# Loading the first rows of x in fewer, taller transfers, and the order of the first norms

## The chip, the cores and the metric

One core of one Trainium2 chip runs the whole kernel in one launch. The metric is the device time of one execution in microseconds (us); the median of three runs of the kernel before is 931.47 us (931.18 to 931.98).

## What is computed

A block of 2048 positions by 512 channels, in float32, goes through two sublayers, each normed, modulated and added back. `B_x` and the inputs' batch of one play no part.

```
mod = (silu(c) @ w_mod).reshape(1, 6, 1, 512)          # sa, ca, ga, sb, cb, gb
h = layernorm(x) * (1 + ca) + sa
a, b = h @ hid_re.T, h @ hid_im.T                      # DFT over the channels
x = x + ga * (seq_re @ a - seq_im @ b)                 # DFT over the positions, real part
h = layernorm(x) * (1 + cb) + sb
z = gelu(h @ w_in)                                     # 512 -> 1792, halves z1 and z2
g = w_sp @ layernorm(z2) + b_sp                        # over the positions
x = x + gb * ((z1 * g) @ w_out)
```

The two 2048 x 2048 matrices of the DFT over the positions, `seq_re` and `seq_im`, are 16 MB each and come from the chip's main memory, as does `x` (4 MB).

## The kernel before, in words

**Precision.** Products are made in a reduced float32 form. Each operand is split in a high part (a copy by ScalarE) and a low part (a difference by VectorE), and three TensorE products (lines 97 to 99) stand for one. The very first step alone (`n` = 0) uses whole float32 operands, line 543, which the profile shows as two passes for each product.

**The first stage.** The order of the sublayer is turned round: the DFT over the positions comes first, on the normed rows. `mm_a(n)`, line 533, is one step of it. For 512 output positions `t`, for the real or the imaginary matrix `j`, and for one tile `s` of 128 rows of x, it adds four products (one for each 128 channels) to four accumulators. Steps 0 to 31 belong to `t` = 0. They take the tiles in groups of four: steps 0 to 3 are the real matrix with tiles 0 to 3, steps 4 to 7 the imaginary one with the same tiles, steps 8 to 15 the tiles 4 to 7, and so on to tile 15. 

**Blocks.** The matrices come in blocks of 512 x 512 (1 MB, tile `stage`, two buffers), one for every four steps. `load` (line 165) issues each block as four transfers of 32 partitions on the sync queue. VectorE turns a quarter of a block by 32 x 32 squares into `t` (line 190). `prep(n)` (line 194) runs two things ahead of the step: `prep_hi(n + 3)`, which turns quarter n + 3 and has ScalarE copy its high part (line 269), and `prep_lo(n + 2)`, in which VectorE makes the low part of quarter n + 2 (line 287). When the last quarter of block b has been turned, block b + 2 is issued.

**Rows of x.** Tile 4g + k holds, in partition 32a + i, row 512g + 128a + 32k + i, to match the turned squares. `load_x` (line 422) brings several k of a group g with one transfer for each a, of 32 partitions. The first two tiles have their own function, `load_two` (line 450): four transfers of 32 partitions for each tile, two issued by the sync queue and two by ScalarE's queue. The first block's first half is issued by the two queues as well, line 161.

**First norms.** `stats_first` (line 436) takes mean and variance on VectorE (lines 439 to 442), the inverse root on GpSimd (line 443), and the product of the two on VectorE for tile 0 and on GpSimd for the others (line 445). `whole_first` (line 458) has ScalarE write tile 0 normed, its channels regrouped, in one activation (line 461), and then a column of ones (line 464). `hi_first` (line 480) writes the high part of a normed tile directly, `norm_x` and `lo_h` give its low part. `keep_busy` (line 365) gives TensorE three float32 products without use while nothing has arrived.

**Order.** The framework adds the waits; it doesn't change the order. Each engine and each DMA queue takes its instructions in the order in which the lines run, so lines 1081 to 1116 are the order of the start, and from line 1117 on `at(n, f, ...)` puts `f` behind step n: `load_x` for the second half of group 1 behind step 0, group 2 behind step 4, group 3 behind step 8, the columns of `w_mod` (tile `wb`, 1 MB each) behind steps 5 and 12; the statistics of later tiles from step 4 on. Lines 1248 to 1253 run the steps.

Of the kernel before, what the change touches and what calls it, by code (L numbers as in the profile page):

```python
# [8 lines left out]
F32 = mybir.dt.float32  # L9
F32R = mybir.dt.float32r  # L10
AF = mybir.ActivationFunctionType
ALU = mybir.AluOpType

P = 128
# [6 lines left out]
def fnet_gmlp_kernel(  # L21
# [32 lines left out]
    nc = tc.nc  # L54
    S, D = x.shape[1:]
    F2 = w_in.shape[1]
    FH = F2 // 2
    Q = 512
    NQ = S // Q
# [4 lines left out]
    x = x.rearrange("b s d -> (b s) d")  # L64
    out = out.rearrange("b s d -> (b s) d")

    def pool(name, side="left", bufs=1):
        return tc.tile_pool(name=name, bufs=bufs, side=side, reuse_waits="tile")
# [11 lines left out]
    def bank(k, name):  # L80
        return psum.tile([P, 512], F32, tag=f"bank{k}", bufs=1, name=name)
# [75 lines left out]
    def load_half(tile_, a, h, engs=(nc.sync,) * 4):  # L157

        v = a.rearrange("(b j) (a s) -> a j b s", j=32, a=4)
        for q in range(4):  # L160
            engs[q].dma_start(tile_[32 * q:32 * q + 32], v[q][:, :, 64 * h:64 * h + 64])
# [3 lines left out]
    def load(b):  # L165
        if b < len(src):
            stage[b] = blocks.tile([P, 16, P], F32, tag="stage", bufs=2, name=f"stage{b}")
            load_block(stage[b], src[b])
        elif b < len(src) + 2:
            j = b - len(src)  # L170
            XB.append(blocks.tile([P, 4, Q], F32, tag="stage", bufs=2, name=f"xb{j}"))
            for g in range(2):
                nc.sync.dma_start(XB[j][:, 2 * g:2 * g + 2], ht_d[g].rearrange("(k p) t -> p k t", p=P)[:, 2 * j:2 * j + 2])
                for kk in range(2):
                    TT[2 * j + kk, g] = XB[j][:, 2 * g + kk]
        elif 4 * (b - NB0) < NE - N4:
            i, gh = divmod(b - NB0, NQ)
            g, h = divmod(gh, 2)
            p = PROD[i]
            stage[b] = blocks.tile([P, 2, 16, 64], F32, tag="stage", bufs=2, name=f"stage{b}")  # L180
            for r in range(2):
                load_half(stage[b][:, r], s_d[S_OF[p], r, g] if p in S_OF else
                          quad(w_sp, r + (2 if p == 4 else 0), g + (2 if p == 1 else 0)), h)
# [5 lines left out]
    def squares(dst, block, k):  # L189
        nc.vector.transpose(dst.rearrange("p (b i) -> p b i", i=32), block[:, :, 32 * k:32 * k + 32])  # L190
# [31 lines left out]
    def form_t(n):  # L222

        if n < N1:
            gg, p, kk = (n - N2) // 4, (n - N2) // 2 % 2, n % 2
            return TT[2 * p + kk, gg]
        p = YPROD[(n - N1) // 4 % len(YPROD)]
        gg, kk = divmod(n % 4, 2)
        a, b, c, d = TT[kk, gg], TT[2 + kk, gg], TT[kk, 2 + gg], TT[2 + kk, 2 + gg]
        return {6: S2[gg, kk], 7: a if n < N3 else c, 4: b if n < N3 else d, 5: c if n < N3 else a, 3: d if n < N3 else b}[p]  # L230
# [21 lines left out]
    def prep_hi(n):  # L252
        if n >= NE or n in highs:
            return
        highs.add(n)
        if N2 <= n < N4:
            T[n] = form_t(n)
        else:
            b, k = divmod(n, 4) if n < N2 else (NB0 + (n - N4) // 4, (n - N4) % 4)
            if b != NB0:  # L260
                T[n] = blocks.tile([P, Q], F32, tag="t", bufs=2, name=f"t{n}")
            if b == NB0:
                assert n in T
            elif n >= N4:
                squares(T[n], stage[b][:, k % 2], k // 2)
            else:
                squares(T[n], stage[b], k)
        AH[n] = SE[2][:, n - N4] if N4 <= n < N4 + 4 else blocks.tile([P, Q], F32R, tag="ah", bufs=4, name=f"ah{n}")
        nc.scalar.activation(AH[n], T[n], AF.Copy)  # L269
        if not N2 <= n < N4 and k == 3:  # L270
            stage.pop(b)
            if b != NB0:
                load(b + 2)


    def prep_lo(n):
        if n >= NE or n in lows:
            return
        lows.add(n)
        if N2 <= n < N4 and n % 4 == 3:  # L280
            AL[n] = slot(0, f"al{n}", F32R) if slots else zrow[0].tile([P, Q], F32R, tag="z1u", bufs=6, name=f"al{n}")
        elif N4 <= n < N4 + 4:
            AL[n] = slot(9 + n - N4, f"al{n}", F32R)
        else:
            AL[n] = blocks.tile([P, Q], F32R, tag="al", bufs=3, name=f"al{n}")
        t = T.pop(n)
        nc.vector.tensor_tensor(AL[n], t, AH[n].bitcast(F32), op=ALU.subtract)  # L287
# [6 lines left out]
    spool = s1.enter_context(pool("spool", "right"))  # L294
# [7 lines left out]
    ones = cpool.tile([P, P], F32, name="ones")  # L302
# [4 lines left out]
    busy = rows.tile([P, D], F32, tag="row", bufs=6, name="busy")  # L307
# [57 lines left out]
    def keep_busy(n, k):  # L365

        ps = bank(k, "busyp")
        for _ in range(n):
            nc.tensor.matmul(ps, ones, busy, start=True, stop=True)

    def fold_sum(t, w, u):

# [46 lines left out]

    X, XG, LN, NRM, h_hi, h_lo = {}, {}, {}, {}, {}, {}  # L420

    def load_x(g, ks=range(4), eng=nc.sync):

        if g not in XG:
            XG[g] = spool.tile([P, 4, D], F32, tag="x", bufs=2, name=f"x{g}")
        k0, k1 = ks[0], ks[-1] + 1
        v = x.rearrange("(g a k i) d -> g a i k d", g=NQ, a=4, i=32)
        for a in range(4):
            eng.dma_start(XG[g][32 * a:32 * a + 32, k0:k1, :], v[g, a][:, k0:k1, :])
        for k in ks:  # L430
            X[4 * g + k] = XG[g][:, k, :]

    def stats_x(s):
# [2 lines left out]
    def stats_first(s):  # L436

        m = spool.tile([P, 12], F32, tag="first", bufs=4, name=f"first{s}")
        nc.vector.bn_stats(m[:, :6], X[s])
        mv = m[:, 8:]  # L440
        nc.vector.bn_aggr(mv[:, :2], m[:, :6])
        nc.vector.tensor_scalar(mv[:, 1:2], mv[:, 1:2], EPS, None, op0=ALU.add)
        nc.gpsimd.tensor_tensor(mv[:, 2:3], mv[:, 1:2], mhalf, op=ALU.pow)
        eng = nc.gpsimd if s else nc.vector
        eng.tensor_scalar(mv[:, 3:4], mv[:, 0:1], mv[:, 2:3], -1.0, op0=ALU.mult, op1=ALU.mult)
        NRM[s] = mv[:, 2:3], mv[:, 3:4]

    two = (nc.sync, nc.sync, nc.scalar, nc.scalar)

    def load_two(k):  # L450
        if not k:
            XG[0] = spool.tile([P, 4, D], F32, tag="x", bufs=2, name="x0")
        v = x.rearrange("(g a k i) d -> g a i k d", g=NQ, a=4, i=32)
        for a in range(4):
            two[a].dma_start(XG[0][32 * a:32 * a + 32, k, :], v[0, a][:, k, :])
        X[k] = XG[0][:, k, :]

    def whole_first(s):

        LN[s] = spool.tile([P, D], F32, tag="xn", bufs=4, name=f"xn{s}")  # L460
        nc.scalar.activation(LN[s].rearrange("p (k a i) -> p k a i", a=4, i=32),
                             X[s].rearrange("p (a k i) -> p k a i", a=4, i=32), AF.Identity,
                             bias=NRM[s][1], scale=NRM[s][0])
        nc.scalar.activation(LN[s][:, :1], ones[:, :1], AF.Copy)

    def split_first(s):
# [7 lines left out]
    def turn_whole(n):  # L474
        T[n] = blocks.tile([P, Q], F32, tag="t", bufs=2, name=f"t{n}")
        squares(T[n], stage[0], n)
        highs.add(n)
        lows.add(n)
# [23 lines left out]
    def ones_x(s):  # L502
        LN[s] = spool.tile([P, D], F32, tag="xn", bufs=4, name=f"xn{s}")
        nc.gpsimd.memset(LN[s][:, 0:1], 1.0)
# [573 lines left out]
            mm([n])  # L1078


    load_two(0)
    stage[0] = blocks.tile([P, 16, P], F32, tag="stage", bufs=2, name="stage0")
    load_half(stage[0][:, :, :64], src[0], 0, two)
    load_two(1)
    nc.scalar.activation(sc, ones[:, :ND], AF.Silu)
    load_x(0, range(2, 4))
    load_half(stage[0][:, :, 64:], src[0], 1)
    load(1)
    load_x(1, range(2))
    keep_busy(3, 5)  # L1090
    ones_x(1)
    ones_x(2)
    ones_x(3)
    stats_first(0)
    whole_first(0)
    turn_whole(0)
    prep_hi(1)
    stats_first(1)
    prep_lo(1)
    hi_first(1)  # L1100
    stats_first(2)
# [13 lines left out]
    rest_first(0)  # L1115
    lo_h(3)
    at(0, load_x, 1, range(2, 4))
    at(2, load_row)
    at(9, silu_row)
# [31 lines left out]
    for j, turn, weigh, row, fold, hi in ((0, (25, 26, 27, 28), (29, 29, 30, 30), 26, (34, 34, 35, 36), (40, 37, 38, 39)),  # L1151
# [8 lines left out]
        n = weigh[3] + 1  # L1160
# [20 lines left out]
    for t in range(NQ):  # L1181
        n = 8 * NQ * (t + 1)
# [136 lines left out]
    for i, p in enumerate(PROD):  # L1319
        for k in range(8):  # L1320
            n = NB[p] + 2 * k
# [11 lines left out]
    for f in range(NF):  # L1333
        n = N4 + 24 + 8 * f
# [109 lines left out]
```

## Time and profile before

| | us |
|---|---|
| median of three runs | 931.47 |
| the profiled execution's own time | 931.31 |
| its span, first to last instruction | 929.5 |
| TensorE products, busy | 923.6 |
| VectorE busy | 736.4 |
| ScalarE busy | 408.7 |
| GpSimd busy | 198.6 |

The profile is one execution; its times are counted from the start of its span. PE is TensorE's products, PEld its weight loads, DVE VectorE, ACT ScalarE, POOL GpSimd, SP the sync engine; a q behind a name is that engine's queue, with the DMA issues. A row of the timeline is start, duration, engine, line, operation, output and inputs; the brackets at its end are the time the engine stood idle before it and what ended that. In the DMA view a queue's row is its packets, the MB it moved and the time of its packets as a share of sixteen DMA engines over the window; an issue's row ends with the median us from issue to landing. A DMA share over 1 means that packets overlap on an engine.

### The profile page before, as it was taken

To read this page: it belongs to the slowest core of one execution; us is meant where nothing else is said; L and a number is where in the kernel's file an instruction comes from. 1 tells how busy PE (TensorE), PEld (TensorE's weight loads), DVE (VectorE), ACT (ScalarE), POOL (GpSimd) and SP (SyncE) were. 2 spreads that over 40 slices of the span, in tenths; PEclk is the share of its full clock that TensorE was granted. 3 is DMA by queue.
4 is the path that set the end of the run, shared out by engine and by line. 5 is a ranking of instruction groups with operands and counts; after the bars stand their busy time and mean duration, and the time that the engine had idled before them with its cause. 6 is when DMAs were issued, how large, how long until landed. Compare 5 with 4: busy or idle time off the path is not lost.

```text
span 929.5 us, 12324 instructions
## 1 busy us (share of the span) xinstructions
PE 923.6 (99%) x4047; PEld 760.1 (82%) x4047; DVE 736.4 (79%) x1216; ACT 408.7 (44%) x733; POOL 198.6 (21%) x375
## 2 busy tenths in 40 slices
PE   9999999999999999999999999999999999999998
PEld 5888888888888888888888888888888888888886
DVE  7799968787687677875678788899799789886762
ACT  5694424232132222322577877674544544331121
POOL 2330000224554165323512321331000000000000
PEclk9999999999999999999999999999999999999999
DMA  9996662857539977996563754444464556734651
GB/s 218 223 225 128 136 158 46 193 150 175 152 98 317 293 215 213 278 343 224 146 216 130 278 196 103 121 105 103 106 144 104 133 140 137 180 102 145 185 178 57
DMA packets 246977, 157.88 MB, mean 170 GB/s; under 512 B 140385, under 2 KB 214369, under 8 KB 246785
## 3 DMA queue, kind: packets, MB, share of 16 engines
q1 hardware_dynamic: 233248, 119.57, 52.3%
q0 software_dynamic: 12272, 36.86, 11.5%
q8 instruction: 32, 0.52, 0.2%
q10 hardware_dynamic: 1392, 0.66, 0.2%
q14 instruction: 33, 0.26, 0.1%
HBM read 120.33 MB, written 36.71 MB: 169 GB/s over the span
## 4 chain that ended last, share of the span: by engine, by line
PE 99%; DMA 0%; ACT 0%; DVE 0%; issue 0%; POOL 0%; ACTq 0%; DVEq 0%; POOLq 0%
PE gp L98 12%; PE gp L97 12%; PE gp L99 12%; PE gw L99 10%; PE gw L97 10%; PE gw L98 10%; PE yp L99 3%; PE yp L97 3%; PE yp L98 3%; PE op L99 3%; PE op L98 3%; PE op L97 3%; PE fp L98 1%; PE fp L99 1%; PE fp L97 1%; PE z2s L98 1%
## 5 line engine op out<-in xcount | busy, mean ns | idle before, releaser
L269 ACT ACTIVATE ah<-t 128x512 fp32r<-128x512 f32 x235 | 148.4, 632 | 362.5 <-DVE t L190 249.8
L287 DVE TENSOR_TENSOR al<-t,ah 128x512 fp32r<-128x512 f32 x235 | 160.2, 682 | 53.0 <-PE gp L98 29.3
L98 PE MATMUL gp<-al,hh 128*128 128x512 f32 x496 | 193.1, 389 | 0.0
L99 PE MATMUL gp<-ah,hl 128*128 128x512 f32 x496 | 193.1, 389 | 0.0
L97 PE MATMUL gp<-ah,hh 128*128 128x512 f32 x496 | 193.1, 389 | 0.0
L190 DVE STREAM_TRANSPOSE t<-stage 128x512 f32<-128x512 f32 x236 | 165.4, 702 | 8.9 <-DMA stage<-in_A_dft_seq_re_dram 3.4
L98 PE MATMUL gw<-al,bh 128*128 128x512 f32 x400 | 155.7, 389 | 0.0
L99 PE MATMUL gw<-ah,bl 128*128 128x512 f32 x384 | 149.6, 390 | 0.0
L97 PE MATMUL gw<-ah,bh 128*128 128x512 f32 x384 | 149.5, 389 | 0.0
L98 PEld LDWEIGHTS gp<-al,hh 128*128 128x128 f32 x496 | 93.1, 188 | 19.4 <-DVE al L287 0.2
L97 PEld LDWEIGHTS gp<-ah,hh 128*128 128x128 f32 x496 | 93.1, 188 | 19.4
L99 PEld LDWEIGHTS gp<-ah,hl 128*128 128x128 f32 x496 | 93.1, 188 | 19.3
L98 PEld LDWEIGHTS gw<-al,bh 128*128 128x128 f32 x400 | 75.1, 188 | 15.5
L99 PEld LDWEIGHTS gw<-ah,bl 128*128 128x128 f32 x384 | 72.1, 188 | 15.3 <-DVE bl L948 0.3
L97 PEld LDWEIGHTS gw<-ah,bh 128*128 128x128 f32 x384 | 72.1, 188 | 15.0
L920 POOL DMA_DIRECT2D s_d<-sj x64 | 35.1, 548 | 107.4 <-DVE sj L912 82.3
L97 PE MATMUL yp<-hth,gh 128*128 128x512 f32 x128 | 49.8, 389 | 0.0
L99 PE MATMUL yp<-hth,gl 128*128 128x512 f32 x128 | 49.8, 389 | 0.0
L98 PE MATMUL yp<-htl,gh 128*128 128x512 f32 x128 | 49.8, 389 | 0.0
L665 POOL DMA_DIRECT2D ht_d<-hturn x62 | 41.0, 667 | 22.9 <-DVE hturn L661 18.2
L97 PE MATMUL op<-woh,uh 128*128 128x512 f32 x112 | 43.6, 389 | 0.0
L99 PE MATMUL op<-woh,ul 128*128 128x512 f32 x112 | 43.6, 389 | 0.0
(240 smaller groups left out, 1442.9 us busy)
## 6 DMA issues: line engine op xcount, KB each, us to landing
stage<-in_A_dft_seq_im_dram SPq DMA_DIRECT2D x64, 256.0 KB, 5.5
sj<-in_B_w_sp_dram SPq DMA_DIRECT2D x32, 512.0 KB, 7.0
s_d<-sj POOLq DMA_DIRECT2D x64, 256.0 KB, 4.3
stage<-s_d SPq DMA_DIRECT2D x128, 128.0 KB, 2.9
stage<-in_A_dft_seq_re_dram SPq DMA_DIRECT2D x60, 256.0 KB, 5.5
stage<-in_B_w_sp_dram SPq DMA_DIRECT2D x88, 128.0 KB, 3.1
wm<-in_w_mod_dram SPq DMA_DIRECT2D x16, 256.0 KB, 6.0
xr<-in_A_x_dram POOLq DMA_DIRECT2D x16, 256.0 KB, 4.7
```

The costliest lines, as they stand in the source:

```text
L97: nc.tensor.matmul(acc, ah, bh, start=first, stop=False, skip_group_check=go_on)
L98: nc.tensor.matmul(acc, ah, bl, start=False, stop=False, skip_group_check=go_on)
L99: nc.tensor.matmul(acc, al, bh, start=False, stop=last, skip_group_check=go_on)
L190: nc.vector.transpose(dst.rearrange("p (b i) -> p b i", i=32), block[:, :, 32 * k:32 * k + 32])
L269: nc.scalar.activation(AH[n], T[n], AF.Copy)
L287: nc.vector.tensor_tensor(AL[n], t, AH[n].bitcast(F32), op=ALU.subtract)
L665: eng.dma_start(v[a, i], ht[32 * a:32 * a + 32].rearrange("c (b r) -> c b r", r=32))
L920: nc.gpsimd.dma_start(s_d[m, r, g][b * P:(b + 1) * P, :], a)
```

## The change

- `load_x` brings each tile k on its own. `engs` lists the queues that share it: with one queue, one transfer of 128 partitions, whose source is four runs of 32 rows; with two, two transfers of 64 partitions, whose sources are two runs of 32 rows each. `load_two` goes. Tiles 0 and 1 use two queues (`two[1:3]`, sync and ScalarE), all later tiles one (sync).
- `whole_first` writes tile 0 normed in two activations of 256 columns each: channels of groups 1 and 2 first, then 0 and 3, by the new `halves`. Step 0 multiplies the groups in the order 1, 2, 3, 0.
- The statistics of tile 1 stand ahead of `prep_hi(1)`, so on VectorE ahead of the turning of quarter 1.
- `keep_busy` takes a list of widths: two products of 512 columns and one of 256 in place of three of 512.

```diff
-        for _ in range(n):
-            nc.tensor.matmul(ps, ones, busy, start=True, stop=True)
+        for w in n:
+            nc.tensor.matmul(ps[:, :w], ones, busy[:, :w], start=True, stop=True)
...
-    def load_x(g, ks=range(4), eng=nc.sync):
+    def load_x(g, ks=range(4), engs=(nc.sync,)):
 
         if g not in XG:
             XG[g] = spool.tile([P, 4, D], F32, tag="x", bufs=2, name=f"x{g}")
-        k0, k1 = ks[0], ks[-1] + 1
-        v = x.rearrange("(g a k i) d -> g a i k d", g=NQ, a=4, i=32)
-        for a in range(4):
-            eng.dma_start(XG[g][32 * a:32 * a + 32, k0:k1, :], v[g, a][:, k0:k1, :])
+        v = x.rearrange("(g a k i) d -> g k a i d", g=NQ, a=4, i=32)
         for k in ks:
+            n = 4 // len(engs)
+            for a, eng in zip(range(0, 4, n), engs):
+                eng.dma_start(XG[g][32 * a:32 * (a + n), k, :], v[g, k, a:a + n])
             X[4 * g + k] = XG[g][:, k, :]
...
-    def load_two(k):
-        if not k:
-            XG[0] = spool.tile([P, 4, D], F32, tag="x", bufs=2, name="x0")
-        v = x.rearrange("(g a k i) d -> g a i k d", g=NQ, a=4, i=32)
-        for a in range(4):
-            two[a].dma_start(XG[0][32 * a:32 * a + 32, k, :], v[0, a][:, k, :])
-        X[k] = XG[0][:, k, :]
+    def halves(h, s):
+
+        v = X[s].rearrange("p (a k i) -> p k a i", a=4, i=32)
+        for ks in (slice(1, 3), slice(0, 4, 3)):
+            nc.scalar.activation(h[:, ks], v[:, ks], AF.Identity, bias=NRM[s][1], scale=NRM[s][0])
 
     def whole_first(s):
 
         LN[s] = spool.tile([P, D], F32, tag="xn", bufs=4, name=f"xn{s}")
-        nc.scalar.activation(LN[s].rearrange("p (k a i) -> p k a i", a=4, i=32),
-                             X[s].rearrange("p (a k i) -> p k a i", a=4, i=32), AF.Identity,
-                             bias=NRM[s][1], scale=NRM[s][0])
+        halves(LN[s].rearrange("p (k a i) -> p k a i", a=4, i=32), s)
         nc.scalar.activation(LN[s][:, :1], ones[:, :1], AF.Copy)
...
-    load_two(0)
+    load_x(0, range(1), two[1:3])
     stage[0] = blocks.tile([P, 16, P], F32, tag="stage", bufs=2, name="stage0")
     load_half(stage[0][:, :, :64], src[0], 0, two)
-    load_two(1)
+    load_x(0, range(1, 2), two[1:3])
     nc.scalar.activation(sc, ones[:, :ND], AF.Silu)
     load_x(0, range(2, 4))
     load_half(stage[0][:, :, 64:], src[0], 1)
     load(1)
     load_x(1, range(2))
-    keep_busy(3, 5)
+    keep_busy((Q, Q, Q // 2), 5)
...
     whole_first(0)
     turn_whole(0)
+    stats_first(1)
     prep_hi(1)
-    stats_first(1)
     prep_lo(1)
```

## The prediction, made before the change was run

> **What bounds the kernel now.** I read the page first, then the chain of waits over the first 20 us, then the busy time by stretch.
>
> ```profile
> span 929.5 us, 12324 instructions
> PE 923.6 (99%) x4047; PEld 760.1 (82%) x4047; DVE 736.4 (79%) x1216; ACT 408.7 (44%) x733; POOL 198.6 (21%) x375
> PE 99%; DMA 0%; ACT 0%; DVE 0%; issue 0%; POOL 0%; ACTq 0%; DVEq 0%; POOLq 0%
> ```
>
> ```profile
> 0.73 0.43 ACTq L455
> 1.19 2.32 DMA x<-in_A_x_dram
> 3.71 0.70 DVE first L439
> 4.96 0.56 POOL first L443
> 5.80 0.82 ACT xn L461
> 6.64 0.21 ACT xn L464
> 6.91 3.67 PE gp L543 x8
> 10.62 8.69 PE gp L549 x36
> ```
>
> ```profile
> 13.57:19.20 5.63, 5.63 (x26) 4.63 (x26) 4.60 (x8) 4.58 (x8) 1.30 (x1) 1.00 1.18 230
> 19.20:50.00 30.80, 30.80 (x137) 25.52 (x136) 24.97 (x45) 18.48 (x35) 9.38 (x31) 1.00 1.17 224
> ```
>
> TensorE is the chain from 6.91 us to the end, and in the two stretches it is busy for their whole length (second number). So the time is the start of the first product that counts, plus a fixed amount of products, plus any hole that appears. The change touches only the first part, and can take back at most some tenths of the 6.91 us; but whatever makes TensorE wait later is added in full. The last two numbers of each stretch are the DMA engines: their mean share is 1.17 to 1.18, at 224 to 230 GB/s. The sixteen engines are full as well; loads run only a little ahead of TensorE. That is the point to watch.
>
> **What the fewer transfers save.** The issuing queue pays per transfer, not per byte:
>
> ```profile
> L455 ACTq DMA_DIRECT2D x<-in_A_x_dram x4: 328/379/440, 0.7 to 3.5; - x4
> L161 ACTq DMA_DIRECT2D stage<-in_A_dft_seq_re_dram x2: 445/493/541, 1.7 to 2.1; - x2
> L155 SPq DMA_DIRECT2D stage<-in_A_dft_seq_re_dram x4: 311/312/451, 13.5 to 16.1; - x4
> ```
>
> 64, 128 and 256 KB, in pieces of 2048, 256 and 512 bytes, all cost 0.3 to 0.5 us of issue (min/median/max in ns). Tile 0 loses one issue on each of two queues, so the half block behind it is issued some 0.43 us earlier. On sync, tiles 2 and 3 lose two more. The later transfers of x are as many as before, or fewer, and their issue lies beside products.
>
> **What the taller transfers may cost.** An issue that lasts 0.31 us for 512 pieces cannot walk through the pieces; something simple must deal them out to the engines. The natural cut is along the outermost index. Before, that index counts 32 on both sides of every load of x, two for each of sixteen engines. In the change the source of `v[g, k, a:a + n]` counts 2 (two queues) or 4 (one) at its outermost, four runs of 32 rows that lie 128 rows apart and so can't be joined. If the cut is there, a transfer runs on two or four engines. No transfer in this trace has such a shape, so its rows can't decide; I take it that the cut is there, and that it begins at the same engine each time.
>
> The Trainium skill, DMA: Bandwidth & Descriptors, section Why a DMA increments its semaphore by 16 and not by 1, says so: the count of engines is the largest up to 16 that divides the slowest dimension of both sides, and on the hardware path they are the lowest-numbered. No run here shows it; by that rule the sum below holds, and without it rival A's.
>
> The price, by rows of the DMA view, for windows of 2.05 to 2.26, 19 to 23 and 75.3 to 82.2 us in that order, and the page's GB/s by slices:
>
> ```profile
> q10 hardware_dynamic: 22, 0.05, 55.0%
> ```
>
> ```profile
> DMA packets 1433, 0.92 MB, mean 230 GB/s; under 512 B 74, under 2 KB 1286, under 8 KB 1433
> ```
>
> ```profile
> q1 hardware_dynamic: 2112, 1.05, 72.7%
> ```
>
> ```profile
> GB/s 218 223 225 128 136 158 46 193 150 175 152 98 317 293 215 213 278 343 224 146 216 130 278 196 103 121 105 103 106 144 104 133 140 137 180 102 145 185 178 57
> ```
>
> The first is ScalarE's queue with rows of x only: 0.55 x 16 engines x 0.21 us / 22 = 84 ns for 2 KB. A run of 32 rows (64 KB) on one engine is then 2.7 us. At the mean of the crowded second window, 230 / 16 = 14.4 GB/s for one engine, it is 4.6 us. I take 2.8, near the first, since twelve engines have none of this load and finish their shares early. A block of 1 MB puts 64 KB of small pieces on each engine: 0.727 x 6.9 = 5.0 us in the third window, at most; 3.1 us at the best slice's 343 GB/s. I take 3.8, about the middle.
>
> Where does this end last? The engine with the most to do is one of the two that carry tiles 0 and 1: both queues' transfers meet there, two runs each per tile. The order of issue up to block 5 is tiles 0 and 1 with the first block, tiles 2 to 7 among blocks 1 to 3, tiles 8 to 11, a block of `w_mod`, block 4, tiles 12 to 15, block 5. On that engine: 4 + 14 = 18 runs, 7 blocks, and a broadcast of c (16 KB, 0.7 us): 18 x 2.8 + 7 x 3.8 + 0.7 = 77.7 us. Before, the tiles put 16 KB each on it, a quarter or an eighth of that.
>
> Fixed latency is to be added:
>
> ```profile
> DMA to landing us min/median/max: 1.9/3.4/6.9
> L190 DVE STREAM_TRANSPOSE t<-stage 128x512 f32<-128x512 f32 x236 | 165.4, 702 | 8.9 <-DMA stage<-in_A_dft_seq_re_dram 3.4
> L269 ACT ACTIVATE ah<-t 128x512 fp32r<-128x512 f32 x235 | 148.4, 632 | 362.5 <-DVE t L190 249.8
> L287 DVE TENSOR_TENSOR al<-t,ah 128x512 fp32r<-128x512 f32 x235 | 160.2, 682 | 53.0 <-PE gp L98 29.3
> ```
>
> ```profile
> 13.58 1.19 PE L549 MATMUL gp<-ah,hh 128*128 128x512 f32 x4
> ...
> 19.15 0.39 PE L97 MATMUL gp<-ah,hh 128*128 128x512 f32 x1
> ```
>
> The quickest transfer of x took 1.9 us from issue to landing, of which 2 x 0.084 on an engine: 1.7 us besides, from an issue at 0.73 us, gives a base of 2.4. Block 5 lands at 2.4 + 77.7 = 80.1. Who waits: VectorE's turning of quarter 20, in `prep(17)`; behind it on the same engine the low part of quarter 19; and TensorE's step 19 needs that. With a turn (0.70), a low part (0.68) and some 0.2 between them, step 19 starts at 81.7. Before, a step is 12 x 30.80 / 136 = 2.72 us (137 products touch that window, its first cut at the edge), and step 4 starts at 19.2, so step 19 at 60.0. The loss is 21.7 us.
>
> It builds up in three places, by the same prices. Tile 0 lands at 2.4 + 2 x 2.8 = 8.0, and the chain from landing to product (3.51 to 6.91) puts step 0 at 11.4. Step 2 needs tiles 0 to 3 and both halves of block 0: 2.4 + 6 x 2.8 + 3.8 = 23.0, and 1.4 us for a turn (0.70) and the high part's copy (0.63): 24.4 in place of 13.6, a loss of 10.8. Then step 15 waits for the low part queued behind block 4's first turn, and step 19 behind block 5's. After that x is on the chip. Block 6 comes after 7.6 us more of loads, for a low part that step 23 needs 10.9 us later, so nothing more is lost, and nothing is caught up: TensorE has no idle time to give.
>
> The bounds: with 2.7 and 3.1, 70.9 us in place of 77.7 and a loss of 15; with 4.6 and 5.0, 118.5 and a loss of 62. The far end needs all sixteen engines to crowd all the time; I stop at runs a fifth dearer than alone and blocks at their dearest, 3.3 and 5.0, which gives 95.1 us and a loss of 39.
>
> **The three small edits.** They move step 0 and step 1.
>
> ```profile
> 1.53 4.77 PE L369 MATMUL busyp<-busy,ones 128*128 128x512 f32 x6 [1.53 <-DVE busy L308]
> 6.05 1.30 DVE L190 STREAM_TRANSPOSE t<-stage 128x512 f32<-128x512 f32 x2 [0.29 <-DMA stage<-in_A_dft_seq_re_dram]
> 7.28 0.65 DVE L439 BATCH_NORM_STATS2 first<-x 128x6 f32<-128x512 f32 x1
> 8.25 0.68 DVE L287 TENSOR_TENSOR al<-t,ah 128x512 fp32r<-128x512 f32 x1
> 9.76 0.81 ACT L483 ACTIVATE hh<-x,first 128x512 fp32r<-128x512 f32 x1 [1.74 <-POOL first L445]
> 3.37 0.34 PEld L369 LDWEIGHTS busyp<-busy,ones 128*128 128x128 f32 x1 [0.52 <-issue]
> 4.22 0.34 PEld L369 LDWEIGHTS busyp<-busy,ones 128*128 128x128 f32 x1 [0.52 <-issue]
> ```
>
> Two halves in place of one activation cost one more fixed part: the one-column activation of the chain takes 0.21, so 0.2 us more in all, but the first two products need the first half alone, after some 0.5 us in place of 0.82. Tile 1's statistics come one turn (0.65) earlier, and the turn, high and low part of quarter 1 one set of statistics (0.65 and two small operations, about 1.0) later. The GpSimd operations that move along pass nothing there: that engine waits for tile 1's statistics only. On ScalarE the high part of tile 1 still stands behind that of quarter 1. The filler's records step by 0.85 us; four of them and two of half width end at 1.53 + 4 x 0.85 + 0.85 = 5.8 in place of 6.3. In the forecast none of this is on the path: step 0 waits for tile 0 until 11.4, tile 1 lands at about 2.4 + 4 x 2.8 + 1.9 = 15.5, and everything up to step 19 is bounded by block 5.
>
> **Rival A: the transfers still spread over sixteen engines.** The cut may go by pieces or by the 64 or 128 partitions of the destination. For it: nothing in the trace shows a narrow transfer. Then the half block lands 0.45 us earlier, the turn at 6.05 moves to 5.6, and the first product to about 6.45, as the filler (5.8) and the first half of tile 0 are ready by then. Step 1 must follow at 6.45 + 3.67 = 10.1: high part of tile 1 at 10.57 - 0.45 - 0.65 = 9.5, quarter 1's low part, which ended at 8.25 + 0.68, at 8.93 - 0.45 + 1.0 = 9.5. Both are in time, so 0.46 us is won: 930.9, between 930.3 and 931.3 with the later steps' waits. It holds as long as tile 0 lands by 6.45 - 2.9 = 3.55 (2.29 from landing to the norm, 0.5 for the half, 0.1 to the product); from there on the start slips one for one. It is the case that is not slower.
>
> **Rival B: narrow, but each transfer begins at another engine.** Then no engine fills up, and only latency counts: tile 0 lands at 2.4 + 2.8 = 5.2 in place of 3.51, and the start slips by 1.7 us to 8.6, with the filler gone since 5.8. If TensorE's clock has dropped by then, eight records at 0.85 in place of 0.46 (3.67 over eight) add 3.1. That gives 933.0 to 936.1, say 934. The Trainium skill, TensorE: Matmul & The Clock Gate, Part 1, has the clock drop after an idle window of about 3.4 us; these 2.8 us would mostly escape it, so by that rule 933.0. No row here shows a drop.
>
> **How the numbers follow.** The profiled execution took 931.31 us, 1.8 beyond its span and 0.16 under the median, so I count from it: 931.3 + 21.7 = 953.0. Its own range is 946 to 970. I give the narrow cut on the same engines 0.78, for the constant issue time and the outermost count; rival A 0.15; rival B 0.05; and 0.02 to a gain above 0.2%, which needs the first product at 5.0 and has no row for it. A measurement of this kernel tells some 0.2% (1.9 us) from no change; so faster 0.02, same 0.15 (A), slower 0.83. To leave out no more than 2 in 10, the range has to take in B's low end, too: 933 to 970.
>
> **What the profile after would show.** Now, tiles 0 and 1 take this long from issue to landing (last number):
>
> ```profile
> x<-in_A_x_dram ACTq DMA_DIRECT2D x4, 64.0 KB, 2.8
> x<-in_A_x_dram SPq DMA_DIRECT2D x4, 64.0 KB, 2.7
> ```
>
> If I am right, these rows show 5 us and more, DMA GB/s over the first 80 us falls under 224 while PE has holes, the first counted product is near 11, step 2 near 24, and from step 23 on PE is full again, with the end moved by the same 20 us. VectorE's waits name DMA of x and stage. I am wrong if x's transfers of 128 KB land within 3 us at the start and the first product is before 7: then A. If step 0 is late by 2 us and nothing after it, B. If the loss is there but the holes come only up to step 4, the later tiles are cheaper than I count.

## The result, and the profile after

The changed kernel takes 967.76 us, the median of 5 runs (966.87 to 969.26), against 931.59 us for the kernel before in the same session (5 runs, 931.18 to 931.98). The ratio is 1.0391, with a 95% interval of 1.0379 to 1.0403: 36.2 us slower. The profiled execution took 968.38 us, 37.1 more than the one before, and its span is 966.5. One execution of one experiment below (e5: 1439 us, at a granted clock of 0.62) was in a slow state and is left out of that experiment's numbers.

The page first: the span, TensorE and its clock by slices, the packets of all DMAs and of the two queues that load x, and the shares of the chain.

```profile
span 966.5 us, 12301 instructions
PE   4885999999999999999999999999999999999998
PEclk9998999999999999999999999999999999999999
DMA packets 246592, 157.88 MB, mean 163 GB/s; under 512 B 140000, under 2 KB 213984, under 8 KB 246400
q1 hardware_dynamic: 232924, 119.57, 49.0%
q10 hardware_dynamic: 1332, 0.66, 0.2%
PE 91%; DMA 5%; SPq 3%; DVE 1%; issue 0%; ACT 0%; DVEq 0%
```

All the loss is in the first four slices of 24 us; after them TensorE is as full as before. The share of the chain that was TensorE's fell from 99% to 91%, and DMA and sync's queue (SPq) have taken it.

The queue rows tell how many engines a transfer uses. The same rows on the page of before:

```profile
q1 hardware_dynamic: 233248, 119.57, 52.3%
q10 hardware_dynamic: 1392, 0.66, 0.2%
```

The MB are equal, so the pieces of data are the same. The page counts 385 packets fewer in all, and 385 fewer under 512 B (140000, before 140385), so what differs are small packets: those that close a transfer, one on each engine that takes part. On ScalarE's queue (q10) four transfers of x became two, and 60 packets are gone: 4 x 16 = 64 became 2 x 2 = 4. On sync's (q1) 24 became 2 of 64 partitions and 14 of 128, and 324 are gone: 24 x 16 = 384 became 2 x 2 + 14 x 4 = 60. So a source that counts 2 at its outermost index runs on two engines, one that counts 4 on four. The rule of the Trainium skill that the prediction cites (DMA: Bandwidth & Descriptors, Why a DMA increments its semaphore by 16 and not by 1) agrees, packet for packet. Which engines they are, no row names.

The same is seen in the bandwidth. These are the 40 slices of the DMA view, tenths of sixteen engines and GB/s, first for 0 to 30 us (slices of 0.75 us), then for 30 to 94 us (1.6 us), with sync's queue over the latter:

```profile
DMA  0001999111113122225522745111442799999999
GB/s 0 0 5 33 226 262 208 38 49 51 49 46 45 56 95 90 100 104 172 136 95 75 189 104 133 52 49 49 127 109 69 222 285 221 247 219 208 209 223 184
```

```profile
DMA  4376325943677222633546639992226344485399
GB/s 89 115 170 141 88 75 120 216 91 132 139 200 187 80 83 90 193 94 123 157 151 150 117 85 240 242 179 74 85 101 180 96 163 120 168 185 99 105 253 211
q1 hardware_dynamic: 13460, 8.88, 54.2%
```

Where a slice shows 1 (from the ninth on), two engines of sixteen work, and they move 46 to 56 GB/s: about 25 GB/s each, 2.6 us for a run of 64 KB. Where it shows 2, four engines move 69 to 104. Between them stand slices of 9 at 179 to 285 GB/s, a block on all sixteen. Sync's queue fills 54% of the engines' time here; the stretches of before had mean shares of 1.17 to 1.18.

That the engines are the same ones for different transfers is seen while both queues load tiles 0 and 1, here from 5.5 to 8 us:

```profile
q1 hardware_dynamic: 37, 0.08, 7.9%
q10 hardware_dynamic: 37, 0.04, 5.2%
```

Both queues move data, and together they take 13.1% of sixteen engines, the time of two. On engines of their own they would take that of four.

The chain of waits over the first 110 us (start, us, what):

```profile
0.73 9.12 DMA x<-in_A_x_dram
9.86 0.54 SPq L430
10.45 2.57 SPq L161
...
16.93 7.32 DMA stage<-in_A_dft_seq_re_dram
...
27.80 4.32 SPq L155
...
37.33 11.54 DMA x<-in_A_x_dram
48.90 0.70 DVE bstx L105
...
69.46 6.77 DMA stage<-in_A_dft_seq_re_dram
76.98 0.66 DVE al L287
78.05 3.23 SPq L155
81.33 3.12 SPq L155
84.50 9.63 DMA stage<-in_A_dft_seq_im_dram
95.60 0.67 PE gp L98
```

Tile 0 lands at 9.85. The chain then runs through sync's own issues, single ones of 2.6 to 4.3 us, to block 0's second half (24.25), tile 7 (48.9), block 4 (76.2) and block 5 (94.1). Up to 95.6 it is a chain of loads, but for products from 51.6 to 63.7; from there on it is one of products. The issues by line, up to 110 us (min/median/max in ns), before and after:

```profile
L155 SPq DMA_DIRECT2D stage<-in_A_dft_seq_im_dram x16: 312/510/1092, 8.8 to 67.2; - x16
```

```profile
L155 SPq DMA_DIRECT2D stage<-in_A_dft_seq_im_dram x16: 487/1174/3762, 20.7 to 105.5; - x16
L155 SPq DMA_DIRECT2D stage<-in_A_dft_seq_re_dram x12: 520/1050/4322, 25.7 to 96.1; - x12
L430 SPq DMA_DIRECT2D x<-in_A_x_dram x16: 541/846/3832, 0.7 to 74.0; - x16
```

A block's quarter, which is unchanged, took 0.5 us to issue and now takes 1.1 to 1.2 in the median and up to 4.3. So the queue is held while the narrow transfers run, and the free engines get little new work from it, as the slices of 1 and 2 show.

The busy time by stretch (length; PE, PEld, DVE, ACT, POOL; granted clock, DMA share, GB/s):

```profile
24.00:50.00 26.00, 20.41 (x78) 15.46 (x78) 14.94 (x27) 10.13 (x17) 5.36 (x15) 0.93 0.69 155
50.00:80.00 30.00, 22.90 (x89) 18.45 (x90) 16.59 (x29) 13.79 (x27) 5.94 (x20) 0.86 0.52 136
80.00:100.00 20.00, 15.31 (x56) 12.10 (x55) 10.61 (x19) 10.69 (x24) 4.27 (x14) 0.86 0.74 174
100.00:130.00 30.00, 30.00 (x134) 24.80 (x133) 28.30 (x49) 18.93 (x43) 3.97 (x12) 1.00 0.74 148
```

From 100 us on TensorE is busy for the whole length again. Up to there neither it nor the DMA engines are (shares of 0.52 to 0.74), and the granted clock is below 1. The starts of single steps (the first product of each), from the timelines, in us:

| step | before | after | later by |
|---|---|---|---|
| 0 | 6.91 | 14.02 | 7.1 |
| 2 | 13.58 | 25.80 | 12.2 |
| 8 | 30.06 | 47.64 | 17.6 |
| 12 | 40.94 | 63.68 | 22.7 |
| 16 | 51.82 | 82.36 | 30.5 |
| 20 | 62.70 | 99.81 | 37.1 |
| 24 | 73.58 | 110.71 | 37.1 |

### The profile page after: what moved, and what is told of

Its sections match the earlier page's. It is cut to its first block, busy times and chain, and to the rows that moved or that the text cites. A ratio compares the mean times of both kernels' runs of the same rounds, so it can differ in the third digit from the quotient of the medians.

```text
span 966.5 us, 12301 instructions
## 1 busy us (share of the span) xinstructions
PE 933.4 (97%) x4047; PEld 764.8 (79%) x4047; DVE 737.3 (76%) x1216; ACT 408.8 (42%) x734; POOL 197.9 (20%) x375
## 4 chain that ended last, share of the span: by engine, by line
PE 91%; DMA 5%; SPq 3%; DVE 1%; issue 0%; ACT 0%; DVEq 0%
PE gp L99 11%; PE gp L98 11%; PE gp L97 11%; PE gw L98 9%; PE gw L99 9%; PE gw L97 9%; PE yp L97 3%; PE yp L99 3%; PE yp L98 3%; PE op L97 3%; PE op L98 3%; PE op L99 3%; DMA x<-in_A_x_dram 2%; SPq L155 2%; DMA stage<-in_A_dft_seq_re_dram 1%; PE fp L97 1%
## 5 line engine op out<-in xcount | busy, mean ns | idle before, releaser
L98 PE MATMUL gp<-al,hh 128*128 128x512 f32 x496 | 196.1, 395 | 13.6 <-DVE al L287 13.6
L99 PE MATMUL gp<-ah,hl 128*128 128x512 f32 x496 | 196.0, 395 | 3.2 <-DVE hl L521 3.2
L97 PE MATMUL gp<-ah,hh 128*128 128x512 f32 x496 | 195.4, 394 | 0.0
L661 POOL DMA_DIRECT2D ht_d<-hturn x62 | 40.9, 665 | 21.7 <-DVE hturn L657 17.8
L98 PE MATMUL op<-wol,uh 128*128 128x512 f32 x112 | 43.6, 389 | 0.0
```

The costliest lines, as they stand in the source:

```text
L97: nc.tensor.matmul(acc, ah, bh, start=first, stop=False, skip_group_check=go_on)
L98: nc.tensor.matmul(acc, ah, bl, start=False, stop=False, skip_group_check=go_on)
L99: nc.tensor.matmul(acc, al, bh, start=False, stop=last, skip_group_check=go_on)
L661: eng.dma_start(v[a, i], ht[32 * a:32 * a + 32].rearrange("c (b r) -> c b r", r=32))
```

## The experiments

The theory after the result: the whole loss comes from the sources' outermost count of 2 or 4, which puts each transfer of x on two or four engines, always the same ones, and holds sync's queue. The rivals: the height or the number of the transfers, the three small edits, engines that change from transfer to transfer, a queue that runs one transfer at a time, the cost of issuing.

**Contiguous rows (e1_contiguous).** As the change, with as many and as tall transfers, but each source is one run of contiguous rows, whose outermost index counts 64 or 128. The rows of x then meet the wrong rows of the matrices; the amount of work is the same.

```diff
-        v = x.rearrange("(g a k i) d -> g k a i d", g=NQ, a=4, i=32)
+        v = x.rearrange("(g k p) d -> g k p d", g=NQ, p=P)
...
-                eng.dma_start(XG[g][32 * a:32 * (a + n), k, :], v[g, k, a:a + n])
+                eng.dma_start(XG[g][32 * a:32 * (a + n), k, :], v[g, k, 32 * a:32 * (a + n)])
```

> The change whole, but each tile takes 128 rows of x that follow one another (row 512g + 128k + p in partition p), so that the source of a transfer counts 64 or 128 at its outermost and not 2 or 4; the rows then meet the wrong rows of the matrices, and the output is not the reference's. Count, size and queue of every transfer stay. Narrow theory (the source's outermost count of 2 or 4 puts a transfer on 2 or 4 engines): the loss is gone, 930.3 to 931.5, the first counted product near 6.5 us, sixteen packets of 4 bytes for each transfer of x. Rival, that fewer and taller transfers cost by themselves (one waits longer for the last of 128 partitions): 960 or more.

933.84 us against 931.49; ratio 1.0025 (1.0016 to 1.0035). Of the 36 us, 34 are gone by this one edit, so neither the height nor the number of the transfers is the cause; the outermost count is. The queues' packets follow:

```profile
q1 hardware_dynamic: 233120, 119.57, 51.4%
q10 hardware_dynamic: 1360, 0.66, 0.3%
```

128 and 32 fewer than before, eight and two transfers less at sixteen each. What is left is a loss of 2.3 us, where a gain of some 0.5 was expected. Its chain:

```profile
1.36 0.83 SPq L161
2.24 4.92 DMA stage<-in_A_dft_seq_re_dram
7.29 0.72 DVE t L190
8.14 5.35 PE gp L539 x8
```

The half block lands at 7.2, and its turn starts at 7.29 in place of 6.05. Its issue gained little: sync took 0.58 us to issue its 128 KB of tile 0, where 64 KB had taken 0.40, and 0.83 in place of 0.42 for the block's first quarter, so the second, on which the turn waits, was issued at 2.24 in place of 2.10. It then took 4.9 us to land. Behind it more is on its way than before: the last of tile 1 is issued at 2.76 in place of 3.53, tile 2 at 3.40 in place of 4.90. The first product is 1.2 us late, and its eight records take 5.35 us in place of 3.67: the clock was at half from 8.12 to 11.53.

**The small edits alone (e2_small_edits).** The loads of before, with the two halves, the earlier statistics and the short filler.

```diff
-    load_x(0, range(1), two[1:3])
+    load_two(0)
...
-    load_x(0, range(1, 2), two[1:3])
+    load_two(1)
...
+        v = x.rearrange("(g a k i) d -> g a i k d", g=NQ, a=4, i=32)
+        for a in range(4):
+            eng.dma_start(XG[g][32 * a:32 * a + 32, k0:k1, :], v[g, a][:, k0:k1, :])
```

> The loads of the kernel before; of the change only the two halves of tile 0, the statistics of tile 1 ahead of the turn, and the shorter filler. Narrow theory: these cost nothing, 930.8 to 931.8, the first counted product between 6.6 and 6.95 us (the half block still lands at 5.9). Rival, that the order or the clock after the shorter filler carries part of the 36 us: 935 or more.

931.65 us against 931.49; ratio 1.0004 (0.9995 to 1.0013). The median shows nothing, in either direction. In the profiled execution (932.74 us) the first product is 0.14 us earlier, and the eight records of step 0 are slower, 5.44 us in place of 3.67; e8 below comes back to this:

```profile
6.77 5.44 PE L547 MATMUL gp<-t,xn 128*128 128x512 f32 x8 [0.63 <-DVE t L190]
```

**Only the first two tiles narrow (e3_first_tiles), only the later ones (e4_later_tiles).** Of the cut, the first part is e3's edit and the second e4's.

```diff
+        if len(engs) == 1:
+            k0, k1 = ks[0], ks[-1] + 1
+            w = x.rearrange("(g a k i) d -> g a i k d", g=NQ, a=4, i=32)
+            for a in range(4):
+                nc.sync.dma_start(XG[g][32 * a:32 * a + 32, k0:k1, :], w[g, a][:, k0:k1, :])
...
+        if len(engs) == 2:
+            k = ks[0]
+            w = x.rearrange("(g a k i) d -> g a i k d", g=NQ, a=4, i=32)
+            for a in range(4):
+                two[a].dma_start(XG[0][32 * a:32 * a + 32, k, :], w[0, a][:, k, :])
...
```

> The change with tiles 2 to 15 loaded as before; tiles 0 and 1 alone in two tall transfers each. Narrow theory with both queues meeting on the same two engines: four runs of 64 KB ahead of step 2, 4 x 3.3 + 4.6 + 1.7 + 2.4 = 21.9, step 2 near 23 in place of 13.6, and nothing lost after it: 939 to 942. If each transfer began at another engine: 933 to 936.

> The change with tiles 0 and 1 loaded as before; tiles 2 to 15 alone in one tall transfer each. Narrow theory, at the prices that the changed kernel shows (3.3 us a run, 4.6 a block): 2.4 + 1.7 + 14 x 3.3 + 7 x 4.6 + 0.7 + 1.6 = 84.8, step 19 there in place of 60.0, and about 1.7 more at half clock: 955 to 959. If each transfer began at another engine, 931 to 934.

The first: 943.07 us, ratio 1.0122 (1.0109 to 1.0136), 11.6 us more, a little over the expected. Step 0 starts at 15.21, step 4 at 30.64, and nothing is lost after it. The second: 959.02 us, ratio 1.0294 (1.0280 to 1.0308), 27.5 more. Its first product is at 6.88, as before, and step 20 is 26.0 us late. 11.6 and 27.5 make 39.1, a little more than the 36.2 of both. The two stretches of each:

```profile
24.00:50.00 26.00, 25.92 (x114) 21.10 (x114) 23.49 (x43) 16.00 (x28) 8.07 (x23) 1.00 1.17 222
50.00:80.00 30.00, 30.00 (x134) 24.87 (x133) 24.57 (x41) 26.38 (x59) 10.50 (x35) 1.00 1.22 221
```

```profile
24.00:50.00 26.00, 20.31 (x75) 15.66 (x74) 14.89 (x27) 9.83 (x17) 4.68 (x16) 0.87 0.52 136
50.00:80.00 30.00, 25.98 (x103) 20.92 (x102) 14.80 (x25) 15.12 (x33) 6.89 (x24) 0.89 0.56 148
```

With the first tiles alone narrow (upper), the engines are full again at 222 GB/s once those are in. With the later ones (lower) they stay at half.

**Two transfers for each later tile (e5_two_on_sync).** Each later tile goes in two transfers of 64 partitions on sync. If every transfer begins at the same engine, the two fullest engines get 14 runs more; if each begins at another, they get none.

```diff
-    def load_x(g, ks=range(4), engs=(nc.sync,)):
+    def load_x(g, ks=range(4), engs=(nc.sync, nc.sync)):
```

> The change with the tiles from 2 on in two transfers each on the sync queue, so that their sources count 2 at the outermost. Narrow theory on the same first engines: each later tile puts two runs on engines 0 and 1 and none on two others: 14 runs more at 2.7 to 3.3 us, 38 to 46 us more than the change, 1006 to 1014. If a transfer begins at another engine each time, the same bytes are spread alike and the time stays near 968. Rival, that the number of issues is the cost: 14 issues of 0.4 us, 973.

1000.83 to 1003.76 us, under the 1006 to 1014 expected; ratio 1.0760 (1.0739 to 1.0782). Against the change's 1.0391 that is 34 us more, 2.5 us for each of the 14 runs. That fits the same engines, a little under the 2.7 that a run takes alone, and excludes other engines each time (968) and a cost of issuing alone (973). A queue that ran one transfer at a time would lose as much here whatever the engines. But in the changed kernel sync's queue moved 649 pieces under 512 B, the half block's, and 28 larger ones, a tile's, side by side from 16.5 to 18 us, and the two queues above share two engines. The DMA view from 30 to 94 us:

```profile
DMA  9921616177111121387256111111111152528329
GB/s 226 202 57 50 188 46 175 45 190 152 43 43 48 50 52 51 134 237 174 69 155 179 45 49 51 51 50 46 51 50 50 68 165 83 140 91 210 97 77 264
```

Nine slices in a row (from the 23rd) at 45 to 51 GB/s: 14 us in which the queue has transfer upon transfer to run and two engines run them all.

**The transfers alone (e6_tall_alone).** The change with all three small edits undone.

```diff
-            nc.scalar.activation(h[:, ks], v[:, ks], AF.Identity, bias=NRM[s][1], scale=NRM[s][0])
+        nc.scalar.activation(LN[s].rearrange("p (k a i) -> p k a i", a=4, i=32),
+                             X[s].rearrange("p (a k i) -> p k a i", a=4, i=32), AF.Identity,
+                             bias=NRM[s][1], scale=NRM[s][0])
...
-    keep_busy((Q, Q, Q // 2), 5)
+    keep_busy((Q, Q, Q), 5)
...
-    stats_first(1)
     prep_hi(1)
+    stats_first(1)
```

> The transfers of the change alone; filler, tile 0's activation and the order of the statistics as before. Narrow theory: 966.5 to 969.5, as the change, since the three small edits lie ahead of the waits for block 4 and block 5. Rival, that the small edits carry a part: 3 us and more under the change.

966.46 us, ratio 1.0373 (1.0358 to 1.0389). The interval overlaps that of the change, and the small edits carry no part that can be told from it. The loss is the transfers'.

**The later tiles on GpSimd's queue (e7_later_on_gpsimd).** Tiles 0 and 1 as before (by the second part of the cut above), the others as in the change, one transfer each, but issued by GpSimd.

```diff
-    def load_x(g, ks=range(4), engs=(nc.sync,)):
+    def load_x(g, ks=range(4), engs=(nc.gpsimd,)):
...
```

> Tiles 0 and 1 loaded as before; tiles 2 to 15 in one tall transfer each, as in the run with the later tiles alone, but issued by GpSimd's queue and not by sync's, so that sync is never held by them. Narrow theory with every transfer of a kind on the same engines: the same bytes on the same four engines, 955 or more. If what costs is that sync's queue is held while it issues (up to 4.3 us for one transfer in the changed kernel), or if this queue deals the transfers out over more engines or begins at another one each time: 932 to 936, the rest by GpSimd's issues ahead of the first inverse root.

947.13 us, ratio 1.0170 (1.0156 to 1.0184): between the two expectations, so the time decides nothing. The issues at the start, the landing (last number) and the queue's row from 6.6 to 11.6 us show what is mixed in it:

```profile
1.33 2.94 POOL L437 DMA_DIRECT2D x<-in_A_x_dram  x4 [0.37 <-issue]
```

```profile
x<-in_A_x_dram POOLq DMA_DIRECT2D x14, 256.0 KB, 11.6
```

```profile
q0 software_dynamic: 579, 0.75, 70.5%
```

GpSimd has nothing to wait for at the start and issues tiles 2 to 5 from 1.33 us on, beside tile 1 and the half block; step 0 slips to 12.77, and step 4 by 8.2 us. One more hole, of 5.6 us, lies in step 10. GpSimd's queue (q0) moved 0.75 MB in those 5 us, 150 GB/s, more than the 104 of four engines above, so the tiles in flight together probably used more than four here, and the narrow cut is probably not all that is lost. Changing the queue also changed the order, and the run doesn't tell what sync's held queue costs.

**The filler's length (e8_small_full_filler, e9_contiguous_full_filler).** The second experiment and the first, each with the filler of before (e9 with the wrong rows, as e1).

```diff
-    keep_busy((Q, Q, Q // 2), 5)
+    keep_busy((Q, Q, Q), 5)
```

> The loads of the kernel before, the two halves and the early statistics, and the filler as before (three products of 512 columns). If the shorter filler lets the clock rise late in some executions: 0.2 to 1 us under the run with the small edits, 930.7 to 931.4. If not: 931.5 to 931.8, no difference.

> The run with contiguous rows (the output is not the reference's, as there), with the filler as before. There, 2.3 us were lost: the first block's first half landed at 7.2 in place of 5.9, and the granted clock was half from 8.1 to 11.5 us. If the clock is the larger part: 931.5 to 932.5 with the longer filler. If the late half block is: 933 to 934, unchanged.

931.62 us, ratio 1.0001 (0.9992 to 1.0010), and 933.15 us, ratio 1.0021 (1.0012 to 1.0030). The first has e2's median, but not its spread: five of e2's eleven executions took 932.1 to 932.7 us, and none of e8's eleven over 931.84. In e2's profiled execution the records of step 0 step by 0.85 us up to 10.3 us, in e8's (931.69) by 0.43. So the shorter filler seems to cost some 0.8 us in some executions, in which the clock comes up later; with one profile of each, that isn't shown. The second is 0.7 us under e1 with overlapping intervals, inside what was expected if the late half block is the larger part; its clock is still at half from 7.9 to 11.3 and its first product at 7.75. The short filler is not what made contiguous rows slower. Whether it is the transfers issued behind the half block was not tried. No version here beats the kernel before.

## Why the prediction was right, and where not

The time was forecast as 953.0 us, with 946 to 970 for this mechanism. The 967.8 measured lies inside, near the dear end (runs of 3.3 and blocks of 5.0, a loss of 39): the mechanism was right, the prices chosen were too low, and the range was wide enough to hold that.

**The cut along the outermost index, always the same engines: right**, and now shown: by the packets, by 25 GB/s an engine, by two queues that share two engines, by e1 (the loss goes with the count) and e5 (34 us for 14 more runs).

**Step 0 at 11.4, step 2 at 24.4: nearly right.** They came at 14.0 and 25.8. Tile 0 landed at 9.85 in place of 8.0, and block 0's first half was turned at 13.16. The sum let step 0 wait for tile 0 alone. But the half block's pieces have to go through the same two engines, which run tiles 0 and 1 at that time (the slices of 1 from 5 to 10.5 us). Step 2's loss was 12.2 for 10.8.

**Block 5's landing at 80.1: the step that failed, by its size.** Block 1's first turn was due at 27.0 by the same prices (2.4, 6 runs, 2 blocks, 0.2) and came at 29.56, 2.6 late. From there to block 5's (94.26) the sum had 12 runs, 5 blocks of 1 MB and the 0.7 of c: 53.3 us. It took 64.7, 11.4 more. Over 17 shares of 64 KB on the fullest engine that is 3.76 us each in place of 3.09. How it divides is not measured: with runs at the 2.7 of a bare two-engine slice, a block took (64.0 - 12 x 2.7) / 5 = 6.3 us, over the 5.0 that the prediction called dearest; with blocks at 4.65 (1.05 MB at the 226 GB/s of before), a run took 3.4. Between them lies any share of waiting. The 2.5 of e5 speaks for cheap runs and dear blocks.

The reason given for the cheap prices, that twelve engines "have none of this load and finish their shares early", fell. They can only be early with work that has been issued. Sync issues in order, and an issue of a block's quarter took up to 4.3 us; so the free engines stood idle (slices of 1 and 2). How much of the 11.4 us is the held queue's and how much the full engines' own, no run separates.

**Three places of loss: wrong in detail.** The holes came in steps 7 and 8 too, as the chain's wait for tile 7 at 48.9 shows; the loss grew with each block (12.2, 17.6, 22.7, 30.5, 37.1).

**A term that the sum didn't have: the clock.** After each long hole the records step by 0.43 us in place of 0.23, in pieces of 3.41 us or a multiple:

```profile
44.56:47.97 3.41, 3.41 (x9) 2.65 (x9) 1.17 (x3) 2.12 (x4) 1.00 (x3) 0.50 0.48 131
75.28:82.11 6.83, 4.42 (x10) 3.51 (x11) 5.73 (x10) 4.86 (x10) 1.50 (x4) 0.50 0.37 117
95.76:99.17 3.41, 3.41 (x9) 2.63 (x10) 3.34 (x6) 2.87 (x6) 1.45 (x4) 0.50 1.12 230
```

The column before the last two is the granted clock. The earlier pieces lie in time that was lost to loads anyhow. The last stands behind the last hole, and eight products there cost 8 x 0.2 = 1.6 us that nothing hides. The prediction priced such a drop for rival B alone. The Trainium skill, TensorE: Matmul & The Clock Gate, Part 1, has windows of 3413 ns at full or half clock; the traces agree in length and level.

So 21.7, 2.6 and 11.4 of loads and 1.6 of clock make 37.3, and the profiled execution lost 37.1.

**Nothing lost after step 23, nothing caught up: right.** Steps 20 and 24 are late by the same 37.1.

**The small edits off the path: right** by the medians (e2, e6, e8).

**Rival A** did not come true, and its own price was wrong. e1 is the rival's case, all else equal: 933.84 in place of 930.9. The sum took the half block to be issued 0.43 us earlier, since an issue cost 0.3 to 0.5 us whatever its size, and to land as much earlier. But tile 0's taller issue took 0.58 us in place of 0.40 and the quarter behind it 0.83 in place of 0.42, so the block's last quarter on sync was issued 0.14 us later, and the block's turn started 1.2 us later.

## What to carry to other kernels

Before transfers are joined, look at the outermost count of both sides as the DMA sees it: rows that do not lie together leave a count of 2 or 4, and the transfer then has two or four engines, the same ones each time. The slices of the DMA view show it at once (tenths of 1 or 2 at some 25 GB/s an engine), and so does the number of packets beside equal bytes. Count the transfers behind a narrow one on its queue as late too, and where loads run barely ahead of TensorE, add the half clock after the last hole.

## What was not expected of the hardware

A narrow transfer delays its queue's next issues: quarters of a block that were issued in 0.5 us took 1.1 to 1.2 in the median and up to 4.3. And fewer, taller transfers need not bring the next one sooner, even with contiguous rows: two issues became one, but the half block's last quarter was issued at 2.24 us in place of 2.10, took 4.9 us to land, and the turn slipped by 1.2 us. Why it took so long is open; more transfers were on their way behind it.
